# Keys and values with a head pair's two heads on separate halves of the partitions, in a linear-attention plus MoE kernel

## The chip, the cores and the metric

The kernel runs on one core of one Trainium2 chip. The metric is the device time of one execution in microseconds (us). Each run also leaves a profile: a trace of one execution, whose span (first to last instruction) is about 2 us shorter than the device time. A core has these engines: PE (TensorE, matmuls), PEld (the weight loads that go with them), DVE (VectorE), ACT (ScalarE), POOL (GpSimd) and SP, which only issues DMA transfers.

## The reference, cut to what matters

```python
# q, k, v: [8 batches, 8 heads, 576 tokens, 64]   w_in: [512, 2048]   w_out: [2048, 512]   float32
q_s = softmax(q, axis=-1)                    # over the 64 channels of a token
k_s = softmax(k, axis=2)                     # over the 576 tokens, for each channel
kv  = einsum('bhsd,bhse->bhde', k_s, v)      # 64 x 64 per head
x   = einsum('bhsd,bhde->bhse', q_s, kv)     # then heads side by side: 4608 tokens x 512
h   = x @ w_in
out = (h * sigmoid(beta * h)) @ w_out     # 4608 x 512
```

The two products with `w_in` and `w_out` are almost all of the arithmetic. The attention is small, but its results `x` are what the products start from.

## The kernel before

The tokens are worked through in nine slabs of 512: slab t is the first 512 tokens of batch t, and slab 8 holds the 64 remaining tokens of all eight batches. A slab has two passes. Pass 1 makes `GT = silu(beta * (x @ w_in))`, 16 tiles of four matmuls (128x512 each); pass 2 makes `GT @ w_out` (with `w_out` divided by `beta` beforehand), 64 matmuls of the same size. The attention of batches 2 to 7 is slipped in between these matmuls. The attention of batch 0 (the "head" of the kernel, before slab 0) and of batch 1 (between slab 0 and slab 1) can't be hidden, because nothing else is ready for PE.

Heads are worked on in four pairs (`hp`). Before the change both heads of a pair lie on the same 128 partitions, four tokens on each, and the 64 tokens that do not fit (576 - 512) are a remainder of their own, loaded with a separate transfer of 256-byte runs:

```python
def load_main(name, th, bufs, b, split=1): ...     # 512 tokens, runs of 4*64 floats = 1024 bytes
def load_rem(name, th, bufs, b): ...               # 64 tokens, runs of 64 floats = 256 bytes

def exp_main(name, srcb, dstb, b, hp0, n):         # one ACT operation per pair, 128x512
    ...
def kv_rows(b, hp, j):                             # j = 0..3 the main rows, j = 4 the remainder
    ...
    # one matmul: 128 key columns (two heads) times 128 value columns (two heads) plus a column of ones
mm(PS[bk][:, 256 * n:256 * n + 129], l, r_[:, 0:129], j == 0, j == 4, ...)
```

The 128x128 product holds the two heads' 64x64 blocks on its diagonal and useless cross products off it. A mask removes those while the result leaves PSUM, and `RC` (one over the sum of the key exponentials) normalises it:

```python
def kvd(b, hp, bk, c):
    add(DVE, lambda e: e.scalar_tensor_tensor(
        KVD[i][:, hp, :], PS[bk][:, c:c + 128], RC[i][:, hp:hp + 1], MASK[:, :],
        ALU.mult, ALU.mult), ...)
```

For batches 0 and 1, which PE waits for, the order is this. `ksum` forms the key sums ahead of the values, with one-column matmuls; then, pair by pair, the values, `KVD`, the product with the transposed q (`QT`), and the copy to `XT`, which is what `w_in` is multiplied with:

```python
def values_now(b, pool, acts):
    for hp in range(NHP + 1):
        if hp < NHP:
            for j in range(5):  mm(PS[bk][:, 0:128], l, r_[:, 0:128], ...)   # values of pair hp
            kvd(b, hp, bk, 0)                                                # DVE
        if hp:
            go(out_step(b, hp - 1, pool, ACTE if hp - 1 in acts else DVE))   # PE, then ACT or DVE
```

`warm(n, bank)` issues n filler matmuls whose result nobody reads; they are meant to keep PE's granted clock up. The program gives each engine one list of instructions, in the order of the code.

The softmax here doesn't subtract the row's maximum and nothing guards it: scores larger than these inputs give would overflow.

Of the kernel before, what the change touches and what calls it, by code (L numbers as in the profile page):

```python
# [12 lines left out]
H = 8  # L13
S = 576
# [10 lines left out]
VW = 2 * D + 2  # L25
# [128 lines left out]
def bass_efficient_attn_shen__then__act_swish_beta_kernel(  # L154
# [12 lines left out]
    with ExitStack() as es:  # L167
# [7 lines left out]
        KF = [sb(f"KF{i}", [128, H, 4, D], F32) for i in range(2)]  # L175
        VF = [sb(f"VF{i}", [128, H, 4, D], F32) for i in range(2)]
        QRF = sb("QRF", [128, H, D], F32)
        KRF = [sb(f"KRF{i}", [128, H, D], F32) for i in range(2)]
        VRF = [sb(f"VRF{i}", [128, H, D], F32) for i in range(2)]
        EQ = [sb(f"EQ{i}", [128, NHP, 4, 2, D], BF16) for i in range(2)]  # L180
        EK = [sb(f"EK{i}", [128, NHP, 4, 2, D], BF16) for i in range(2)]
        EQR = sb("EQR", [128, H, D], BF16)
        EKR = [sb(f"EKR{i}", [128, H, D], BF16) for i in range(2)]
# [4 lines left out]
        VB = [sb(f"VB{i}", [128, 4, NHP, VW], BF16) for i in range(2)]  # L188
        VR = [sb(f"VR{i}", [128, NHP, VW], BF16) for i in range(2)]
# [18 lines left out]
        MASK = sb("MASK", [128, 128], F32)  # L208
# [21 lines left out]
        add(DVE, lambda e: e.memset(MASK[:, :], 0.0), w=["mask0"])  # L230
        add(DVE, lambda e: e.memset(MASK[0:64, 0:64], 1.0), r=["mask0"], w=["mask1"])
        add(DVE, lambda e: e.memset(MASK[64:128, 64:128], 1.0), r=["mask0"], w=["mask2"])

        def homes(i):
            add(POOL, lambda e: e.memset(VB[i][:, :, :, 2 * D:VW], 1.0), w=[("vone", i)])
            for p in (0, 32, 64, 96):
                add(POOL, lambda e, p=p: e.memset(
                    VR[i][p:p + 32, :, 2 * D:VW], 1.0 if 32 <= p < 96 else 0.0),
                    w=[("vrone", i, p)])
            for p in (0, 96):  # L240
                add(POOL, lambda e, p=p: e.memset(KRF[i][p:p + 32, :, :], 0.0), w=[("krf0", i, p)])
                add(POOL, lambda e, p=p: e.memset(VRF[i][p:p + 32, :, :], 0.0), w=[("vrf0", i, p)])

# [17 lines left out]
        def load_rem(name, th, bufs, b):  # L261
            i = b % 2
            a = bass.AP(th, b * H * S * D + SM * D, [[D, SR], [S * D, H], [1, D]])
            add(SP, lambda e: e.dma_start(bufs[i][32:96, :, :], a), w=[(name, i)],
                slot=f"{name}{i}")
# [7 lines left out]
        def load_k(b, split=1):  # L273
            load_rem("krf", kt_h, KRF, b)
            load_main("kf", kt_h, KF, b, split)

        def load_v(b, split=1):
            load_rem("vrf", vt_h, VRF, b)
            load_main("vf", vt_h, VF, b, split)

# [8 lines left out]
        def exp_main(name, srcb, dstb, b, hp0, n):  # L289
            i = b % 2  # L290
            for hp in range(hp0, hp0 + n):
                o = bass.AP(dstb[i], hp * 512, [[2048, 128], [64, 2], [128, 4], [1, 64]])
                a = bass.AP(srcb[i], hp * 512, [[2048, 128], [256, 2], [64, 4], [1, 64]])
                add(ACTE, lambda e, o=o, a=a: e.activation(o, a, ACT.Exp),  # L294
                    r=[(name + "f", i, hp)], w=[("e" + name, i, hp)])

        def exp_q(b, hp0=0, n=4):
            exp_main("q", QF, EQ, b, hp0, n)

        def exp_k(b, hp0=0, n=4):  # L300
            exp_main("k", KF, EK, b, hp0, n)

        def exp_kr(b):
            i = b % 2
            add(ACTE, lambda e: e.activation(EKR[i][:, :, :], KRF[i][:, :, :], ACT.Exp),
                r=[("krf", i), ("krf0", i, 0), ("krf0", i, 96)], w=[("ekr", i)])
# [25 lines left out]
        def cast_v(b, hp, eng=POOL):  # L332
            i = b % 2
            o = bass.AP(VB[i], hp * VW, [[4 * NHP * VW, 128], [NHP * VW, 4], [64, 2], [1, 64]])
            a = bass.AP(VF[i], hp * 512, [[2048, 128], [64, 4], [256, 2], [1, 64]])
            add(eng, lambda e: (e.copy if eng == ACTE else e.tensor_copy)(o, a),  # L336
                r=[("vf", i, hp), ("vone", i)], w=[("vb", i, hp)])

        def cast_vr(b, eng=POOL):
            i = b % 2  # L340
            o = bass.AP(VR[i], 0, [[NHP * VW, 128], [VW, NHP], [1, 2 * D]])
            a = bass.AP(VRF[i], 0, [[H * D, 128], [2 * D, NHP], [1, 2 * D]])
            add(eng, lambda e: e.tensor_copy(o, a),  # L343
                r=[("vrf", i), ("vrf0", i, 0), ("vrf0", i, 96)], w=[("vr", i)])
# [35 lines left out]
        def kv_rows(b, hp, j):  # L380
            i = b % 2
            if j < 4:
                return (bass.AP(EK[i], hp * 512 + j * 128, [[2048, 128], [1, 128]]),
                        VB[i][:, j, hp, :], [("ek", i, hp)], [("vb", i, hp)], [("vone", i)])
            return (bass.AP(EKR[i], hp * 128, [[512, 128], [1, 128]]), VR[i][:, hp, :],
                    [("ekr", i)], [("vr", i)], [("vrone", i, p) for p in (0, 32, 64, 96)])

        def kvd(b, hp, bk, c):
            i = b % 2
            add(DVE, lambda e: e.scalar_tensor_tensor(  # L390
                KVD[i][:, hp, :], PS[bk][:, c:c + 128], RC[i][:, hp:hp + 1], MASK[:, :],
                ALU.mult, ALU.mult),
                r=[("ps", bk), ("rc", i, hp), "mask0", "mask1", "mask2"], w=[("kvd", i, hp)],
                bank=[bk])

        def kv_steps(b, hps, pool=MB):
# [3 lines left out]
            def one(n, hp, j):  # L400
                if n == 0 and j == 0:
                    st["b"] = bank(pool)
                bk = st["b"]
                l, r_, ke, kv, ko = kv_rows(b, hp, j)
                mm(PS[bk][:, 256 * n:256 * n + 129], l, r_[:, 0:129], j == 0, j == 4,
                   r=ke + kv, w=[("ps", bk)], bk=bk)
                if n == len(hps) - 1 and j == 4:
                    for m, h2 in enumerate(hps):
                        s_ = PS[bk][:, 256 * m + 128:256 * m + 129]
                        add(DVE, lambda e, s_=s_, h2=h2: e.reciprocal(RC[i][:, h2:h2 + 1], s_),  # L410
                            r=[("ps", bk)], w=[("rc", i, h2)], bank=[bk])
                        kvd(b, h2, bk, 256 * m)
            return [lambda n=n, hp=hp, j=j: one(n, hp, j) for n, hp in enumerate(hps)
                    for j in range(5)]

        def out_mm(b, hp, bk):
            i = b % 2
            mm(PS[bk][:, :], KVD[i][:, hp, :], QT[i][:, hp, :], True, True,
               r=[("kvd", i, hp), ("qt", i, hp)], w=[("ps", bk)], bk=bk)
# [41 lines left out]
        def outr_steps(b):  # L461
# [3 lines left out]
            def one(hp, e_):  # L465
                if hp == 0 and e_ == 0:
# [4 lines left out]
                   True, True, r=[("kvd", e_, hp), "qtr"], w=[("ps", bk)], bk=bk)  # L471
# [6 lines left out]
        def attn(b):  # L478
            s = spread(kv_steps(b, (0, 1)) + kv_steps(b, (2, 3)), 8, 36)
# [26 lines left out]
        def ksum(b, hp, kb):  # L506
            for j in range(5):
                l, r_, ke, kv, ko = kv_rows(b, hp, j)
                mm(PS[kb][:, hp:hp + 1], l, r_[:, 128:129], j == 0, j == 4, r=ke + ko,
# [7 lines left out]
        def values_now(b, pool, acts):  # L517
            i = b % 2
            for hp in range(NHP + 1):
                if hp < NHP:  # L520
                    bk = bank(pool)
                    for j in range(5):
                        l, r_, ke, kv, ko = kv_rows(b, hp, j)
                        mm(PS[bk][:, 0:128], l, r_[:, 0:128], j == 0, j == 4, r=ke + kv,
# [32 lines left out]
        wgate = []  # L557
        warm(8, 0)
        exp_q(0)
        for hp in range(NHP):  # L560
            norm_main(0, hp, 1, POOL if hp % 2 else DVE)
        for c in range(8):
            a = bass.AP(win_h, 256 * c, [[DFF, 128], [128 * DFF, NM], [1, 256]])
            add(POOL, lambda e, c=c, a=a: e.dma_start(WIN[:, :, 256 * c:256 * c + 256], a),
                w=[("win", c)], slot=f"win{c}", after=P.writer[("kf", 0, 3)] if c == 0 else ())
            if c == 1:
                cast_vr(0)
            if c == 4:
                wgate.append(P.ops[-1])
        homes(1)  # L570
        kb = bank(HEAD)
        go(t_steps(0, (0,), HEAD, ACTE))
        warm(3, 0)
        go(t_steps(0, (1,), HEAD, ACTE))
        warm(2, 0)
        exp_kr(0)
        exp_k(0, 0, 1)
        go(t_steps(0, (2,), HEAD, ACTE))
        warm(3, 0)
        exp_k(0, 1, 2)  # L580
        ksum(0, 0, kb)
        warm(3, 0)
        ksum(0, 1, kb)
        warm(1, 0)
        go(t_steps(0, (3,), HEAD, ACTE))
        warm(2, 0)
        bb = bank(HEAD)
        mm(PS[bb][:, 0:NF], BT[:, :], IDF[:, :], True, True, r=["bt", "idf"], w=[("ps", bb)],
           bk=bb, tr=True)
        add(DVE, lambda e: e.tensor_scalar(BC[:, :], PS[bb][:, 0:NF], -1e-20, None, ALU.is_gt),  # L590
            r=[("ps", bb)], w=["bc0"], bank=[bb])
        add(DVE, lambda e: e.scalar_tensor_tensor(BC[:, :], PS[bb][:, 0:NF], 1e-20, BC[:, :],
                                                  ALU.is_lt, ALU.mult),
            r=[("ps", bb), "bc0"], w=["bc"], bank=[bb])
        add(DVE, lambda e: e.scalar_tensor_tensor(BETA[:, :], BC[:, :], 4e-20, PS[bb][:, 0:NF],
# [183 lines left out]
```

## Time and profile before

Median 292.86 us (292.64 to 292.89). The profiled execution has a span of 290.5 us.

| | before |
|---|---|
| start of the values of batch 0 | 14.29 us |
| first matmul of slab 0's pass 1 / pass 2 | 17.11 / 31.27 us |
| key sums of batch 1, start | 45.98 us |
| values of batch 1, start | 47.56 us |
| first matmul of slab 1 | 51.21 us |
| last matmul | 286.24 us |
| landing of the last chunk of Q, K, V of batch 0 | 6.56, 10.70, 14.09 us |

All times are from the start of the span. (The 6.75 us that the prediction below gives for Q is the landing of the small `beta` load just behind it.) First the page of the profile: busy time, share of the span and number of instructions of each engine; the DMA packets by size; and the chain of work that ended last, by engine.

```profile
PE 281.4 (97%) x1499; PEld 133.1 (46%) x1499; DVE 114.0 (39%) x225; ACT 165.9 (57%) x251; POOL 44.1 (15%) x77
...
DMA packets 58291, 47.32 MB, mean 163 GB/s; under 512 B 26001, under 2 KB 54689, under 8 KB 57249
...
PE 94%; DVE 2%; DMA 1%; ACT 0%; POOL 0%; issue 0%; POOLq 0%
```

The kernel is bound by PE: the chain is PE for 94%. A change can then win only by giving PE less to do, or by making PE wait less where it does wait, and these places are the head and batch 1's attention.

Next, some groups of instructions by their shapes: line, engine, operation, output<-input, shapes and count, then the busy time in us and the mean duration in ns, then the idle time before them.

```profile
L357 PE MATMUL PS<-WOUT,GT 128*128 128x512 bf16 x576 | 133.2, 379 | 0.0
L357 PE MATMUL PS<-XT,WIN 128*128 128x512 bf16 x576 | 132.3, 379 | 0.8 <-ACT XT L427 0.7
...
L357 PE MATMUL PS<-VB,EK 128*128 128x129 bf16 x96 | 20.3, 220 | 0.0
...
L294 ACT ACTIVATE EK<-KF 128x512 bf16<-128x512 f32 x32 | 18.0, 617 | 0.6 <-DMA KF<-in_k_dram 0.2
...
L390 DVE SCALAR_TENSOR_TENSOR KVD<-PS,RC,MASK 128x128 bf16<-128x128 f32 x32 | 10.9, 349 | 2.1 <-PE PS L357 1.0
```

A mean duration is not the cost of one more instruction where instructions overlap. The large matmuls last 379 ns each but start every 216 ns; a 129-column matmul lasts 220 ns and adds 57 ns. For that reason costs below are differences of start times, and PE's busy time, a sum of overlapping stretches, is not used.

The key exponentials of batch 0 on ACT and the two ends of slab 0's pass 1 on PE, from the timeline (start, length of the merged stretch, engine, line, what, count):

```profile
9.75 0.62 ACT L294 ACTIVATE EK<-KF 128x512 bf16<-128x512 f32 x1
...
10.73 1.16 ACT L294 ACTIVATE EK<-KF 128x512 bf16<-128x512 f32 x2
...
13.10 0.63 ACT L294 ACTIVATE EK<-KF 128x512 bf16<-128x512 f32 x1
...
17.11 14.33 PE L357 MATMUL PS<-XT,WIN 128*128 128x512 bf16 x64
...
31.27 4.91 PE L357 MATMUL PS<-WOUT,GT 128*128 128x512 bf16 x22
```

And batch 1's attention: the end of the key sums, the fillers, the start of the values, slab 1.

```profile
46.46 0.16 PE L357 MATMUL PS<-VR,EKR 128*128 128x1 bf16 x1
46.49 1.24 PE L357 MATMUL PS<-WARM 128*128 128x512 bf16 x5
47.56 0.39 PE L357 MATMUL PS<-VB,EK 128*128 128x128 bf16 x4
...
51.21 3.01 PE L357 MATMUL PS<-XT,WIN 128*128 128x512 bf16 x13 [0.68 <-ACT XT L427]
```

### The profile page before, as it was taken

The page shows a single profiled execution, that of the slowest core. Times are in us where ns is not written, and L with a number is a line of the kernel's source. Part 1 is how long each engine was busy: PE and PEld are TensorE (multiplying, and loading weights), DVE is VectorE, ACT ScalarE, POOL GpSimd, SP SyncE. Part 2 cuts the span into 40 slices and gives each one's busy share as a digit, 9 for nine tenths or more (in the row PEclk, how much of TensorE's full clock was granted, in tenths as well). Part 3 has the DMA queues.
Part 4 walks back from the last instruction along what each step waited for, and adds up shares of the span by engine and source line. Part 5 has one row for each costly group of instructions (what it writes and reads, how often), then busy time and mean ns, then how long its engine had stood idle before and what let it go on. Part 6 is the DMA issues. An engine that isn't in the chain of part 4 may idle for free.

```text
span 290.5 us, 3750 instructions
## 1 busy us (share of the span) xinstructions
PE 281.4 (97%) x1499; PEld 133.1 (46%) x1499; DVE 114.0 (39%) x225; ACT 165.9 (57%) x251; POOL 44.1 (15%) x77
## 2 busy tenths in 40 slices
PE   6899998999999999999999999999999999999994
PEld 2444445444545444544454445444544444444441
DVE  4430596215686046505580557044904400110011
ACT  5777572979767852787268716891670086017500
POOL 5780015034541300210012000000000000000000
PEclk9799999999999999999999999999999999999999
DMA  6999999999999989506980016000900030012022
GB/s 200 306 179 318 383 327 292 343 363 286 323 337 322 204 246 347 96 2 186 331 225 2 1 54 165 0 1 18 206 13 0 2 144 0 2 54 90 0 74 72
DMA packets 58291, 47.32 MB, mean 163 GB/s; under 512 B 26001, under 2 KB 54689, under 8 KB 57249
## 3 DMA queue, kind: packets, MB, share of 16 engines
q1 hardware_dynamic: 53728, 44.45, 52.1%
q0 software_dynamic: 4224, 2.10, 5.6%
q10 hardware_dynamic: 320, 0.52, 0.6%
q8 instruction: 12, 0.20, 0.3%
q14 instruction: 7, 0.05, 0.1%
HBM read 36.71 MB, written 9.44 MB: 159 GB/s over the span
## 4 chain that ended last, share of the span: by engine, by line
PE 94%; DVE 2%; DMA 1%; ACT 0%; POOL 0%; issue 0%; POOLq 0%
PE PS L357 93%; PE PS L355 1%; DMA QF<-in_q_dram 1%; DVE XT L427 1%; DVE QS L319 0%; DVE KVD L390 0%; POOL EQ L321 0%; DVE O2S L633 0%; DVE EQ L321 0%; ACT EQ L294 0%; ACT XT L427 0%; DVE QI L320 0%; POOLq L137 0%
## 5 line engine op out<-in xcount | busy, mean ns | idle before, releaser
L628 ACT ACTIVATE GT<-PS,BETA 128x512 bf16<-128x512 f32 x144 | 98.5, 687 | 87.6 <-PE PS L357 87.6
L357 PE MATMUL PS<-WOUT,GT 128*128 128x512 bf16 x576 | 133.2, 379 | 0.0
L357 PE MATMUL PS<-XT,WIN 128*128 128x512 bf16 x576 | 132.3, 379 | 0.8 <-ACT XT L427 0.7
L357 PEld LDWEIGHTS PS<-WOUT,GT 128*128 128x128 bf16 x576 | 54.5, 98 | 62.3
L357 PEld LDWEIGHTS PS<-XT,WIN 128*128 128x128 bf16 x576 | 53.5, 98 | 62.3 <-ACT XT L427 1.0
L633 DVE COPY O2S<-PS 128x512 f32<-128x512 f32 x34 | 23.3, 688 | 112.9 <-PE PS L357 112.8
L357 PE MATMUL PS<-VB,EK 128*128 128x129 bf16 (+2 forms) x160 | 24.9, 209 | 0.0
L319 DVE TENSOR_REDUCE QS<-EQ 128x8 f32<-128x512 bf16 (+1 forms) x22 | 20.0, 909 | 7.7 <-ACT EQ L294 7.7
L427 DVE CAST XT<-PS 128x512 bf16<-128x512 f32 x27 | 18.6, 690 | 11.3 <-PE PS L357 11.2
L294 ACT ACTIVATE EQ<-QF 128x512 bf16<-128x512 f32 x32 | 18.1, 620 | 6.7 <-DMA QF<-in_q_dram 6.3
L336 POOL CAST VB<-VF 128x512 bf16<-128x512 f32 x28 | 18.1, 648 | 9.5 <-DMA VF<-in_v_dram 7.4
L294 ACT ACTIVATE EK<-KF 128x512 bf16<-128x512 f32 x32 | 18.0, 617 | 0.6 <-DMA KF<-in_k_dram 0.2
L357 PEld LDWEIGHTS PS<-VB,EK 128*128 128x128 bf16 x160 | 13.2, 98 | 8.7 <-ACT EK L294 0.7
L321 DVE TENSOR_TENSOR EQ<-EQ,QI 128x1024 bf16<-128x1024 bf16 (+1 forms) x14 | 15.8, 1129 | 0.5
L343 POOL CAST VR<-VRF 128x512 bf16<-128x512 f32 x8 | 4.9, 616 | 66.4 <-PE PS L357 53.4
L321 POOL TENSOR_TENSOR EQ<-EQ,QI 128x512 bf16<-128x512 bf16 x8 | 8.3, 1043 | 32.1 <-DVE QI L320 31.9
L357 PE MATMUL PS<-QT,KVD 128*128 128x512 bf16 x32 | 11.9, 381 | 0.7 <-DVE KVD L390 0.7
L357 PE MATMUL PS<-WARM 128*128 128x512 bf16 x30 | 10.7, 481 | 1.2 <-DVE WARM L221 1.2
L390 DVE SCALAR_TENSOR_TENSOR KVD<-PS,RC,MASK 128x128 bf16<-128x128 f32 x32 | 10.9, 349 | 2.1 <-PE PS L357 1.0
L355 PE MATMUL PS<-IDB,EQ 128*128 128x128 bf16 x48 | 6.3, 234 | 2.5 <-DVE EQ L321 1.6
L357 PE MATMUL PS<-VR,EKR 128*128 128x129 bf16 (+2 forms) x40 | 8.2, 208 | 0.0
L551 DVE TENSOR_SCALAR WOUT<-WST,RB 128x512 bf16<-128x512 f32 x8 | 3.3, 482 | 11.6 <-DMA WST<-in_moe_w_out_dram 11.6
(55 smaller groups left out, 98.9 us busy)
## 6 DMA issues: line engine op xcount, KB each, us to landing
out_dram<-O2S SPq DMA_DIRECT2D x8, 1024.0 KB, 5.1
QF<-in_q_dram SPq DMA_DIRECT2D x6, 1024.0 KB, 8.5
KF<-in_k_dram SPq DMA_DIRECT2D x6, 1024.0 KB, 8.8
VF<-in_v_dram SPq DMA_DIRECT2D x6, 1024.0 KB, 8.8
QF<-in_q_dram SPq DMA_DIRECT2D x8, 256.0 KB, 6.9
KF<-in_k_dram SPq DMA_DIRECT2D x8, 256.0 KB, 5.6
VF<-in_v_dram SPq DMA_DIRECT2D x8, 256.0 KB, 5.7
WIN<-in_moe_w_in_dram POOLq DMA_DIRECT2D x8, 256.0 KB, 6.3
```

Of the source, the lines that this page charges most:

```text
L294: add(ACTE, lambda e, o=o, a=a: e.activation(o, a, ACT.Exp), r=[(name + "f", i, hp)], w=[("e" + name, i, hp)])
L319: add(DVE, lambda e: e.tensor_reduce(s_, a, AX.X, ALU.add), r=ks, w=[("qs", i, hp0)])
L321: add(eng, lambda e: e.tensor_tensor(a, a, vb, ALU.mult), r=ks + [("qi", i, hp0)], w=ks)
L336: add(eng, lambda e: (e.copy if eng == ACTE else e.tensor_copy)(o, a), r=[("vf", i, hp), ("vone", i)], w=[("vb", i, hp)])
L343: add(eng, lambda e: e.tensor_copy(o, a), r=[("vrf", i), ("vrf0", i, 0), ("vrf0", i, 96)], w=[("vr", i)])
L355: add(PE, lambda e: e.transpose(o, l, r_), r=r, w=w, bank=[bk])
L357: add(PE, lambda e: e.matmul(o, l, r_, start=start, stop=stop), r=r, w=w, bank=[bk])
L390: add(DVE, lambda e: e.scalar_tensor_tensor(KVD[i][:, hp, :], PS[bk][:, c:c + 128], RC[i][:, hp:hp + 1], MASK[:, :], ALU.mult, ALU.mult), ...
L427: add(eng, lambda e: (e.copy if eng == ACTE else e.tensor_copy)(XT[i][:, hp, :], PS[bk][:, :]), r=[("ps", bk)], w=[("xt", i, hp)], bank=[bk])
L551: add(DVE, lambda e, f=f: e.tensor_scalar(WOUT[:, f, :], STAGE[c][:, f % 4, :], RB[:, f:f + 1], None, ALU.mult), r=SKEY[c] + ["rb"], w=[(" ...
L628: add(ACTE, lambda e: e.activation(GT[:, f, :], PS[bk][:, :], ACT.Silu, scale=BETA[:, f:f + 1]), r=[("ps", bk), "beta"], w=[("gt", f)], ba ...
L633: add(eng, lambda e: (e.copy if eng == ACTE else e.tensor_copy)(O2S[t % 2][:, u, :], PS[bk][:, :]), r=[("ps", bk)], w=[("o2", t % 2, u)], ...
```

## The change

The two heads of a pair go to 64 partitions each, nine tokens on every partition (64 x 9 = 576). There is no remainder of keys or values any more, and the runs in memory are 2304 bytes long. To keep the heads apart in one matmul, the key exponentials are written block-diagonally into a tile that is zero elsewhere: the upper head into columns 0 to 63, the lower into 64 to 127. The product then has only 64 value columns, and no mask is needed. Cut to its core:

```diff
-VW = 2 * D + 2
+NG = S // 64
+VW = D + 2
+KW = NG * D
@@
-        EK = [sb(f"EK{i}", [128, NHP, 4, 2, D], BF16) for i in range(2)]
+        EK = [sb(f"EK{i}", [128, NHP, NG, 2 * D], BF16) for i in range(2)]
@@ (homes) zeros off the diagonal, once, on POOL
+                z = EK[i][64 * e_:64 * e_ + 64, :, :, 64 * (1 - e_):64 * (2 - e_)]
+                add(POOL, lambda e, z=z: e.memset(z.bitcast(F32), 0.0), w=[("ekz", i, e_)])
@@ (exp_k) two operations of 64 partitions per pair; step=2 (two pairs at once) from batch 2 on
+            for hp in range(hp0, hp0 + n, step):
+                hps = range(hp, hp + step)
+                for e_ in range(2):
+                    o = bass.AP(EK[i], 64 * e_ * NHP * NG * 128 + hp * NG * 128 + 64 * e_,
+                                [[NHP * NG * 128, 64], [128, NG * step], [1, 64]])
+                    a = bass.AP(KF[i], 64 * e_ * NHP * KW + hp * KW,
+                                [[NHP * KW, 64], [64, NG * step], [1, 64]])
+                    add(ACTE, lambda e, o=o, a=a: e.activation(o, a, ACT.Exp), ...)
@@ (kvd) two operations of 64 partitions in place of one masked one per pair; from batch 2 on
@@       one such operation covers two or four pairs
+            for e_ in range(2):
+                o = bass.AP(KVD[i], 64 * e_ * NHP * 128 + hp * 128 + 64 * e_, ...)
+                add(DVE, lambda e, o=o, a=a, s_=s_: e.tensor_tensor(o, a, s_, ALU.mult), ...)
@@ (kv_steps, ksum, values_now) nine matmuls per pair in place of five, of half the width
-                mm(PS[bk][:, 256 * n:256 * n + 129], l, r_[:, 0:129], j == 0, j == 4, ...)
+                mm(PS[bk][:, VW * n:VW * n + D + 1], l, r_[:, 0:D + 1], j == 0, j == NG - 1, ...)
@@ (head) two w_in loads issued one key chunk earlier, ahead of Q's last pair on POOL;
@@        q transposes copied by DVE, one V cast more on DVE, all XT copies on ACT, four fillers fewer
+        load_win(0)
+        load_win(1)
...
-        values_now(0, HEAD, (1, 3))
+        values_now(0, HEAD, (0, 1, 2, 3))
```

## The prediction

It was written before anything of the change was built or run.

> **What bounds the kernel.** The chain of waits is PE for 94% of a 290.5 us span. In the two large products a 128x512 matmul starts every 216 ns (matmul starts in the trace); 1152 of them, 249 us, are untouched. From 17.8 to 286.6 us PE is fed without a gap except around batch 1's attention (45.8 to 51.2 us, 4.3 us busy). Only the head (0 to 17.8 us) and the attention matmuls between the large ones can give.
>
> **Matmuls.** Per batch 20 matmuls of 129 columns become 36 of 65. In the trace a 129-column one adds 57 ns between large ones; a 64-column one (QTR,KVD) 28 ns; the weight load stays hidden in both. So 20 x 57 = 1.14 us becomes 36 x 29 = 1.04 us: about 0.6 us over six batches. The key sums of batches 0 and 1 are one-column matmuls at 25 ns; 36 instead of 20 cost 0.4 us more each. The Trainium skill (page "TensorE: Matmul & The Clock Gate", section "Back-to-back issue gap") gives a floor of about 25 ns; the trace agrees. On PE alone: nearly nothing.
>
> **ScalarE.** Back to back, a 512-element exponential takes 0.52 us, a 1-element one 0.20 us: about 0.1 us plus 0.83 ns per element. Half-filled partitions double the elements: keys cost 8 x 0.58 = 4.6 us in batches 0 and 1 and 4 x 1.06 = 4.2 us later, against 2.6 us with the remainder. ScalarE is 57% busy; only slab 1's second pass is tight (two batches' exponentials, 66.5 to 77.8 us before; to about 81.4 after on the old clock, just when the last XT copy is wanted). At most 0.3 us lost there.
>
> **DMA and head.** The head is a stream of loads: Q has landed at 6.75, K at 10.70, V at 14.09 us; the first full product starts at about 17.8 us. Runs of 1024 B move 256 KB in 0.75 us (350 GB/s), the 256 B remainders 128 KB in 0.50 us (262 GB/s), the w_out loads with 2048 B runs 1 MB in 2.7 us (387 GB/s). With 2304 B runs and no remainders K and V should take about 3.0 us each: V lands at 12.8 to 13.3 us. ScalarE loses four QT copies to DVE but gains 2 us of exponentials, which end near 12.3 us (13.7 before). Mask memsets, remainder casts and four filler matmuls leave; all XT copies go to ScalarE, so DVE no longer holds up KVD. I estimate the first full product near 16.2 us: 1.6 us saved.
>
> **Batch 1.** Its loads land about 2 us earlier, so they keep up with the earlier PE; its key exponentials end just when slab 0's second pass does. Key sums +0.4 us, perhaps 0.1 us for the last pair's EQ.
>
> **Sum.** -1.6 (head) +0.5 (batch 1) -0.6 (interleaved) +0.1 (slab 1) = -1.6 us: 291.2 us, range 289.8 to 292.6. Chances: faster by over 2% 0.02, within 2% 0.96, slower 0.02.
>
> **What would show it.** Start to first full product shorter by 1 to 2 us; V landing before 13.5 us; starts after a 65-column matmul spaced near 29 ns; ScalarE busy time up by about 13 us without PE waiting for it; DMA packets from 58,000 to about 42,000; the rest within 0.5 us of before.
>
> **What would make it wrong.** The granted clock is 0.5 from 7.6 to 11.0 us after a thin stretch; fewer fillers could move or add such a stretch (up to +1.7 us). PE waiting for key exponentials in batches 0 or 1, or slab 2's first activations delayed. The w_in loads, issued one key chunk earlier, could slow V. Half-partition operations could cost more than the same columns on 128.

## More of the kernel before

```profile
48.04 0.63 DVE L390 SCALAR_TENSOR_TENSOR KVD<-PS,RC,MASK 128x128 bf16<-128x128 f32 x2 [1.00 <-PE PS L357]
...
49.49 0.60 DVE L390 SCALAR_TENSOR_TENSOR KVD<-PS,RC,MASK 128x128 bf16<-128x128 f32 x2
```

Two masked KVD operations take 0.60 us together although one lasts 0.35: the second starts before the first has ended.

## The result, and the profile after

The changed kernel took 293.83 us (293.14 to 294.42, four runs) against 292.86 us (four runs with the one of that round). Ratios here are the mean time of one kernel's fast runs over that of the other's in the same rounds, so not quite the ratio of the medians quoted: 1.0029, 95% interval 1.0011 to 1.0047. It is within 2%, as forecast, but slower and not faster, and outside the predicted range of 289.8 to 292.6 us. A second set of six runs on another chip (e6 below) gave 1.0013 (0.9991 to 1.0034). The honest result is "nothing gained, perhaps 0.1 to 0.3% lost".

The same lines of the page for the changed kernel, whose profiled span is 292.0 us:

```profile
PE 279.4 (96%) x1623; PEld 133.5 (46%) x1655; DVE 112.1 (38%) x206; ACT 181.5 (62%) x248; POOL 42.3 (14%) x61
...
DMA packets 41652, 47.33 MB, mean 162 GB/s; under 512 B 17553, under 2 KB 29857, under 8 KB 40609
...
PE 81%; DMA 8%; SPq 4%; ACT 2%; POOL 1%; issue 1%; DVE 1%
```

The packets fell as forecast. ACT became 15.6 us busier. The chain is no longer 94% PE: loads, and ACT's exponentials, now stand in it. The groups:

```profile
L346 PE MATMUL PS<-VB,EK 128*128 128x65 bf16 x216 | 32.2, 193 | 0.4
L301 ACT ACTIVATE EK<-KF 64x1152 bf16<-64x1152 f32 x24 | 27.8, 1158 | 0.4
...
L301 ACT ACTIVATE EK<-KF 64x576 bf16<-64x576 f32 x16 | 10.9, 681 | 2.3 <-DMA KF<-in_k_dram 2.0
...
L383 DVE TENSOR_TENSOR KVD<-PS,RC 64x64 bf16<-64x64 f32 x16 | 3.6, 222 | 2.1 <-PE PS L346 1.7
```

The head:

```profile
8.20 5.62 ACT L301 ACTIVATE EK<-KF 64x576 bf16<-64x576 f32 x8 [0.39 <-DMA KF<-in_k_dram]
...
17.36 14.33 PE L346 MATMUL PS<-XT,WIN 128*128 128x512 bf16 x63
...
31.53 4.70 PE L346 MATMUL PS<-WOUT,GT 128*128 128x512 bf16 x21
```

The eight exponentials follow each other without a pause for 5.62 us, 0.70 to 0.71 us from start to start, and end at 13.82 us. In the kernel before they ended at 13.73 us although they began 1.5 us later. Batch 1's attention, PE and then DVE:

```profile
46.23 1.25 PE L346 MATMUL PS<-VB,EK 128*128 128x1 bf16 x36
47.35 1.24 PE L346 MATMUL PS<-WARM 128*128 128x512 bf16 x5
48.43 0.71 PE L346 MATMUL PS<-VB,EK 128*128 128x64 bf16 x18
...
52.77 1.47 PE L346 MATMUL PS<-XT,WIN 128*128 128x512 bf16 x6 [0.68 <-ACT XT L421]
```

```profile
48.93 0.98 DVE L383 TENSOR_TENSOR KVD<-PS,RC 64x64 bf16<-64x64 f32 x4 [1.08 <-PE PS L346]
...
50.67 0.98 DVE L383 TENSOR_TENSOR KVD<-PS,RC 64x64 bf16<-64x64 f32 x4
```

The four half KVD operations of two pairs take 0.98 us, where two masked ones took 0.60 to 0.63: one lasts 0.22 us, and they start 0.25 us apart. They do not overlap at all.

So the two profiled executions differ, stage by stage (starts of matmuls in the traces):

| stage | before, us | after, us | difference |
|---|---|---|---|
| to slab 0's pass 2 (the head, and pass 1 of slab 0) | 31.27 | 31.53 | +0.26 |
| pass 2 of slab 0, to batch 1's key sums | 14.71 | 14.70 | -0.01 |
| key sums of batch 1 (start to the first filler) | 0.51 | 1.12 | +0.61 |
| fillers | 1.07 | 1.08 | +0.01 |
| values of batch 1 to the first matmul of slab 1 | 3.65 | 4.34 | +0.69 |
| slab 1, pass 1 | 14.36 | 14.48 | +0.12 |
| slab 1, pass 2, to the last matmul | 220.67 | 220.49 | -0.18 |
| sum (last matmul) | 286.24 | 287.74 | +1.50 |

In these two traces the loss is made up of the attention of batches 0 and 1; the whole rest gains 0.06 us. One trace is one execution: in a second trace of the changed kernel (e6 below) slab 0's pass 2 starts at 31.03 us, 0.24 us before the kernel before, so the sign of the head's term is not shown. That the forecast 1.6 us were not gained is.

### The profile page after: what moved, and what is told of

It reads as the page before. It is cut to its first block, busy times and chain, and to the rows that moved or that the text cites. A ratio compares the mean times of both kernels' runs of the same rounds, so it can differ in the third digit from the quotient of the medians.

```text
span 292.0 us, 3977 instructions
## 1 busy us (share of the span) xinstructions
PE 279.4 (96%) x1623; PEld 133.5 (46%) x1655; DVE 112.1 (38%) x206; ACT 181.5 (62%) x248; POOL 42.3 (14%) x61
## 2 busy tenths in 40 slices
DMA packets 41652, 47.33 MB, mean 162 GB/s; under 512 B 17553, under 2 KB 29857, under 8 KB 40609
## 4 chain that ended last, share of the span: by engine, by line
PE 81%; DMA 8%; SPq 4%; ACT 2%; POOL 1%; issue 1%; DVE 1%
PE PS L346 81%; DMA KF<-in_k_dram 5%; SPq L251 3%; DMA WIN<-in_moe_w_in_dram 2%; ACT EK L301 2%; SPq L540 1%; POOL WIN L555 1%; DVE KVD L383 1%; PE PS L344 0%; POOL EQ L317 0%; SPq L261 0%; DVE O2S L633 0%; ACT XT L421 0%; SPq L530 0%
## 5 line engine op out<-in xcount | busy, mean ns | idle before, releaser
L346 PE MATMUL PS<-WOUT,GT 128*128 128x512 bf16 x562 | 131.8, 379 | 0.6
L346 PEld LDWEIGHTS PS<-XT,WIN 128*128 128x128 bf16 x576 | 54.9, 98 | 63.1 <-ACT XT L421 1.6
L301 ACT ACTIVATE EK<-KF 64x1152 bf16<-64x1152 f32 (+1 forms) x40 | 38.7, 967 | 2.7 <-DMA KF<-in_k_dram 2.0
L346 PE MATMUL PS<-VB,EK 128*128 128x65 bf16 (+2 forms) x360 | 38.1, 187 | 1.9 <-ACT EK L301 0.8
L332 POOL CAST VB<-VF 128x576 bf16<-128x576 f32 x28 | 21.2, 757 | 74.4 <-DMA VF<-in_v_dram 42.4
L346 PEld LDWEIGHTS PS<-VB,EK 128*128 128x128 bf16 x360 | 24.2, 97 | 9.6 <-ACT EK L301 1.4
L421 DVE CAST XT<-PS 128x512 bf16<-128x512 f32 x25 | 17.2, 691 | 11.0 <-PE PS L346 10.9
L346 PE MATMUL PS<-QT,KVD 128*128 128x512 bf16 x29 | 11.1, 381 | 1.3 <-DVE KVD L383 0.9
L346 PE MATMUL PS<-WARM 128*128 128x512 bf16 x25 | 9.1, 483 | 1.2 <-DVE WARM L219 1.2
L383 DVE TENSOR_TENSOR KVD<-PS,RC 64x64 bf16<-64x64 f32 (+2 forms) x30 | 8.9, 298 | 2.5 <-PE PS L346 1.7
L344 PEld LDWEIGHTS PS<-IDB,EQ 128*128 128x128 bf16 x48 | 4.1, 105 | 6.2 <-issue 2.4
```

Source lines behind the costliest of these rows:

```text
L301: add(ACTE, lambda e, o=o, a=a: e.activation(o, a, ACT.Exp), r=[("kf", i, h) for h in hps], w=[("ek", i, h, e_) for h in hps])
L332: add(eng, lambda e: (e.copy if eng == ACTE else e.tensor_copy)(o, a), r=[("vf", i, hp), ("vone", i)], w=[("vb", i, hp)])
L344: add(PE, lambda e: e.transpose(o, l, r_), r=r, w=w, bank=[bk])
L346: add(PE, lambda e: e.matmul(o, l, r_, start=start, stop=stop), r=r, w=w, bank=[bk])
L383: add(DVE, lambda e, o=o, a=a, s_=s_: e.tensor_tensor(o, a, s_, ALU.mult), r=[("ps", bk)] + [("rc", i, h) for h in hps], w=[("kvd", i, h, ...
L421: add(eng, lambda e: (e.copy if eng == ACTE else e.tensor_copy)(XT[i][:, hp, :], PS[bk][:, :]), r=[("ps", bk)], w=[("xt", i, hp)], bank=[bk])
```

## The experiments

Theories at the start. S: the half-filled exponentials on ScalarE hold up the key sums. K: the halved KVD operations on VectorE lengthen the chain from values to XT. D: batch 1's first key chunk lands late (in the changed kernel at 41.41 us, where 15 of its 16 parts had landed by 39.93) and holds up everything behind it.

The table holds the stages of the traces that the argument uses, in us from the start of the span. One trace is one execution; the same changed kernel (after, e6) differs by 0.5 us between its two. The runs e1 to e4 had one chip, e6 to e9 another, the f and g runs a third. Two columns hardly move between traces of one kernel and carry most of the argument: "values 1 to slab 1" (V1) and "values 0 to the head's end" (V0; the head's end is the start of slab 0's pass 2 less the 13.82 us that 64 matmuls of 216 ns take, so it is right only where pass 1 does not stall). V0 also takes in waits for other things than KVD: for `w_in` and RC in f1 (0.19 and 0.39 us), for `w_in` in e1 (0.41 us), for RC in f3 (0.71 us).

| run | values 0 | pass 2 of slab 0 | key sums 1 | values 1 | slab 1 | last matmul | V0 | V1 |
|---|---|---|---|---|---|---|---|---|
| before | 14.29 | 31.27 | 45.98 | 47.56 | 51.21 | 286.24 | 3.16 | 3.65 |
| after | 14.33 | 31.53 | 46.23 | 48.43 | 52.77 | 287.74 | 3.38 | 4.34 |
| e6, after again | 13.83 | 31.03 | 45.93 | 48.05 | 52.40 | 287.36 | 3.38 | 4.35 |
| e1, one exponential per pair | 13.64 | 31.07 | 47.16 | 49.14 | 53.49 | 288.34 | 3.61 | 4.35 |
| e2, masked KVD | 14.20 | 31.13 | 45.84 | 47.96 | 51.63 | 286.60 | 3.11 | 3.67 |
| e3, before with halved exponentials | 16.59 | 33.58 | 48.29 | 49.87 | 53.52 | 288.67 | 3.17 | 3.65 |
| f1, masked KVD, zigzag | 13.91 | 31.24 | 47.59 | 50.05 | 53.73 | 288.57 | 3.51 | 3.68 |
| f2, f1 without fillers | 13.57 | 30.51 | 45.29 | 47.22 | 50.90 | 285.74 | 3.12 | 3.68 |
| f3, e1 with Q's last pair first | 12.71 | 30.62 | 45.79 | 47.77 | 52.12 | 286.97 | 4.09 | 4.35 |
| f4, f3 with half of w_out | 12.14 | 30.32 | 45.02 | 47.01 | 51.35 | 286.20 | 4.36 | 4.34 |
| g1, before without fillers | 14.11 | 31.15 | 46.12 | 47.11 | 50.87 | 285.89 | 3.22 | 3.76 |
| g2, f2 again | 14.05 | 30.98 | 46.49 | 47.51 | 51.40 | 286.24 | 3.11 | 3.89 |

### e1: one exponential per key pair

```diff
-                for e_ in range(2):      # batches 0 and 1: two operations on 64 partitions
+                o = bass.AP(EK[i], hp * NG * 128, [[NHP * NG * 128, 128], [128, NG], [1, 64]])
+                a = bass.AP(KF[i], hp * KW, [[NHP * KW, 128], [64, NG], [1, 64]])   # 128 partitions
```

The lower head's exponentials land in the wrong columns, so the result is wrong (the tile's other columns are set to ones to keep sums finite).

> The changed kernel with the key exponentials of batches 0 and 1 as four operations on 128 partitions (576 elements each) in place of eight on 64; the result is wrong on purpose, every later operation stays. Theory S (ScalarE: half-filled exponentials hold up the key sums): exponentials of batch 0 end near 11.2 us instead of 13.8, those of batch 1 near 44.5 instead of 47.1; the first full product starts about 1.0 us earlier than in the changed kernel (18.2 us), the first product of slab 1 about 1.8 us earlier (52.8 us), in all near 292.0 us. Rival K (only the doubled KVD operations on VectorE cost): less than 0.3 us gained, near 293.6 us. Rival D (a late first key chunk of batch 1 from DMA, last of 16 engines at 41.4 us): no gain in batch 1 beyond what the head gives.

Measured: 293.90 us, ratio 1.0013 (0.9979 to 1.0046). Batch 0's exponentials ended at 11.00 us instead of 13.82, and batch 1's at 45.03 instead of 47.05. So the part of S about ScalarE is right, and yet hardly anything was gained. In the head the values started only 0.69 us earlier (0.19 us earlier than in e6): the transposes of Q's last pair, whose normalisation POOL does after issuing two `w_in` loads, were ready at 12.69 us only, and behind the values PE waited for the first `w_in` chunk, which in this run landed at 17.20 us. In batch 1 a wait appeared that the changed kernel did not have, as the timeline of PE shows:

```profile
43.50 0.40 PE L353 MATMUL PS<-IDB,EQ 128*128 128x128 bf16 x4 [0.76 <-POOL EQ L326]
...
46.06 0.40 PE L353 MATMUL PS<-IDB,EQ 128*128 128x128 bf16 x4 [0.22 <-POOL EQ L326]
```

PE waits for the normalised Q of batch 1 (EQ), which came late because the loads were late. Theory S alone falls: the exponentials are one of several paths of nearly equal length.

### e2: KVD of a pair in one masked operation

```diff
+            if n == 1:                                   # batches 0 and 1
+                a = bass.AP(PS[bk], c, [[512, 128], [0, 2], [1, 64]])   # the 64 columns, read twice
+                m = bass.AP(MASK, 0, [[128, 128], [64, 2], [1, 64]])
+                add(DVE, lambda e: e.scalar_tensor_tensor(
+                    o, a, RC[i][:, hp:hp + 1], m, ALU.mult, ALU.mult), ...)
```

> The changed kernel with KVD of one pair made by one masked operation on 128 partitions, reading the 64 PSUM columns twice, as the kernel before does with 128 columns; only in the attention of batches 0 and 1; the result is right. Rival K (KVD in two halves, 0.25 us each, not overlapped, in the chain values-KVD-output-XT): each of the two stages shorter by 0.3 to 0.5 us, total near 293.0 us. If KVD is not on the chain: same as the changed kernel, 293.8 us. Theory S alone (ScalarE) expects at most 0.2 us.

Measured: 293.14 us, ratio 0.9992 (0.9956 to 1.0029), result right. From the DVE timeline and the PE timeline of batch 1:

```profile
48.47 0.66 DVE L387 SCALAR_TENSOR_TENSOR KVD<-PS,RC,MASK 128x128 bf16<-128x128 f32 x2 [1.01 <-PE PS L351]
```

```profile
51.64 2.55 PE L351 MATMUL PS<-XT,WIN 128*128 128x512 bf16 x11 [0.68 <-ACT XT L436]
```

V1 is 3.67 us, that of the kernel before, against 4.34 or 4.35 in every trace that has the halves; V0 is 3.11 against 3.38. f2 and g2 below, with the masked KVD too, have V0 of 3.12 and 3.11. Theory K holds: halving KVD costs 0.68 us in batch 1 and 0.27 us in the head, 0.95 us in all. The sign of the total agrees, but the interval of the time is wider than the effect; the stages show it, not the totals.

### e3: the kernel before with its key exponentials halved

```diff
-                o = bass.AP(dstb[i], hp * 512, [[2048, 128], [64, 2], [128, 4], [1, 64]])
+            for e_ in range(2):                          # batches 0 and 1
+                p = 64 * e_ * 2048
+                o = bass.AP(EK[i], p + hp * 512, [[2048, 64], [64, 2], [128, 4], [1, 64]])
```

> The kernel before with one part of the change alone: the key exponentials of batches 0 and 1 each split into two operations on 64 partitions (512 elements, dense layout, right result). Theory S: 8 x 0.65 us or so in place of 4 x 0.52 to 0.62; head longer by 1.5 to 2.3 us (first full product 19.3 to 20 us instead of 17.8), batch 1 hardly longer since its keys land 0.6 us earlier there (0 to 0.4 us); total near 294.6 us (+0.6%). If half-filled exponentials are harmless: 292.9 us.

Measured: 294.78 us, ratio 1.0049 (1.0019 to 1.0079). The values of batch 0 started at 16.59 us instead of 14.29, and from there on each stage was as before, but for 0.12 us in slab 1's first pass. In the ACT timeline two of these exponentials merge into 1.27 us:

```profile
9.50 1.27 ACT L311 ACTIVATE EK<-KF 64x512 bf16<-64x512 f32 x2
```

One of them lasts 627 ns, so they did not overlap. In the head of the kernel before, halving costs 2.3 us. The changed kernel offsets most of this by starting the exponentials 1.5 us earlier (no key remainder, and no QT copies on ACT).

### e4: the exponentials ordered by half

```diff
-            for hp in range(hp0, hp0 + n, step):
-                hps = range(hp, hp + step)
-                for e_ in range(2):
+            for e_ in range(2):
+                for hp in range(hp0, hp0 + n, step):
```

> The changed kernel with the key exponentials of a batch ordered by half: all of partitions 0 to 63, then all of 64 to 127, right result. If it is the change of the partition half from one operation to the next that stops two operations from overlapping: starts within one half are spaced 0.58 us (576 elements) and 1.07 us (1152) in place of 0.706 and 1.18. If half-filled operations never overlap: 0.70 and 1.18 stay. Time within 0.5 us of the changed kernel either way.

The four exponentials of a later batch, in the changed kernel and then in e4:

```profile
103.26 4.70 ACT L301 ACTIVATE EK<-KF 64x1152 bf16<-64x1152 f32 x4
```

```profile
105.27 4.44 ACT L301 ACTIVATE EK<-KF 64x1152 bf16<-64x1152 f32 x4
```

Start to start, e4's are 1.06 us apart within a half and 1.17 us where the half changes; the changed kernel's are always 1.18 us apart. In batch 0 the second half's follow each other at 0.57 to 0.59 us, and the changed kernel's at 0.70. So it is the change of the start partition from one operation to the next that costs 0.11 to 0.13 us, not the half-filled operation as such. The time was 295.83 us in its single run, about 2 us more than the changed kernel, against the expectation: batch 0's first key sums now wait for the second half, and the records of the granted clock show 0.5 from 14.0 to 17.4 us, in the middle of the values.

### e6: the changed kernel again; e7, e8, e9: three versions with an edit too many

e6 is the changed kernel itself, run as a control on the chip of e7 to e9.

> The changed kernel as it is, run again as a control beside the next three on their chip. Expected 293.9 us (ratio to before near 1.003), with the values of batch 0 starting near 14.3 us and the first product of slab 1 at 52.8 us, as in its first trace; how far these move tells how much one trace is worth.

Measured: 293.56 us, ratio 1.0013 (0.9991 to 1.0034); slab 1 started at 52.40 us. V0 and V1 repeat to 0.01 us; the rest moved by 0.3 to 0.5 us. The exponentials of batch 0 took 5.62 us again, and began and ended 0.50 us earlier (7.70 and 13.32 us), because the first key chunk landed at 7.67 us instead of 8.18; the values followed, at 13.83 instead of 14.33.

The three others shared an edit that was meant to bring batch 1's loads forward: the first `w_out` load waits for the third `w_in` chunk instead of the fifth (`if c == 2` in place of `if c == 4` where the gate is set). e7 is e1 with it and with Q's last pair normalised ahead of the `w_in` loads, e8 has the masked KVD and the zigzag order of f1 below, and e9 is e8 without the five fillers.

> The run with one exponential per key pair (wrong on purpose), and two more waits taken away: GpSimd normalises Q's last pair ahead of the first w_in loads, and the w_out loads follow the third w_in load, not the fifth. Theory P (three paths of nearly equal length end in the head's values: key exponentials, Q's last pair on GpSimd, V's last chunk; and two in batch 1: key exponentials, and the load stream w_in, w_out, Q): values of batch 0 start near 12.5 to 13.0 us (14.3 changed kernel, 13.6 with the one exponential alone); first product of slab 1 near 51.7 us (53.5 with the one exponential alone); total near 292.3 us. If the exponentials were the only cause, the two extra edits do nothing: values at 13.6, slab 1 at 53.5, 293.9 us.

> The changed kernel, right result, with the causes mended that earlier runs showed: KVD of one pair in one masked operation, key exponentials in an order that changes the partition half four times per batch instead of seven, w_out loads behind the third w_in load. Expected: exponentials of batch 0 end near 13.4 us (13.8), values start near 13.9 us, values to first product of slab 1 3.67 us (4.35), that product near 51.2 us (before 51.2, changed 52.8); total 0.2 to 0.9 us under the changed kernel, about equal to before (ratio 0.998 to 1.001).

> The last one without the five filler matmuls between batch 1's key sums and values. If the fillers, not the V casts, hold the values there: 1.0 us more saved, the first product of slab 1 near 50.2 us, total near 292.1 us, ratio to before near 0.997. If V's last chunk or the clock holds them: nothing, or a stretch at half clock shows.

Measured: 295.86, 294.66 and 294.32 us, ratios 1.0079, 1.0053 and 1.0036. All three missed for one reason, which e8's list of PE's waits shows (us in total, times, longest):

```profile
PE PS L351 <- DMA WIN<-in_moe_w_in_dram: 2.8, 2, 2.4
```

The `w_out` loads took bandwidth from the `w_in` loads, and slab 0's pass 1 starved. I had thought that the `w_in` stage left bandwidth free. It does not: the profile's DMA queue counts 2.1 MB for it, which is what it writes as bf16, but it reads 4.2 MB of fp32 (36.7 MB read from HBM in all are Q, K and V with 28.3, and the two weights with 4.2 each). In e8 its last chunk landed at 32.19 us, instead of 25.30. The early part of e7 is still of use: with the exponentials and Q's last pair both out of the way, the values started at 12.57 us (predicted there: 12.5 to 13.0).

### f1 and f2: the two mends without that edit

f1 is the changed kernel with e2's KVD and with

```diff
-                for e_ in range(2):
+                for e_ in ((0, 1), (1, 0))[hp // step % 2]:      # "zigzag"
```

and f2 leaves out `warm(5, 3)` ahead of batch 1's values as well.

> The changed kernel, right result, with two mends and the w_out loads where they were (moving them up starved the w_in loads: PE stalled over 3 us in slab 0): KVD of one pair in one masked operation, and key exponentials in the order that changes the partition half four times. Theory (KVD halves and exponentials that do not overlap are most of the loss): values to first product of slab 1 3.67 us, that product at 51.2 to 51.6 us, total 0.7 to 1.1 us under the changed kernel, ratio to before 0.997 to 1.000. If the control's closeness to before (1.0013) means that there is nothing to mend: ratio 1.001.

> The last one without the five filler matmuls between batch 1's key sums and values (1.08 us of PE). If the fillers hold the values: 0.9 to 1.1 us less, first product of slab 1 near 50.4 us, ratio near 0.995. If V's last chunk (48 us) and its cast hold them: 0.3 to 0.5 us less.

f1: 293.60 us, ratio 0.9996 (0.9967 to 1.0025). f2: 292.29 us, ratio 0.9962 (0.9931 to 0.9993), the first version whose interval lies below 1 (its repeat, g2 below, does not confirm that). In f1's trace the third chunk of batch 1's Q landed 2.3 us after the second (0.75 us is usual), and PE stood idle 0.72 and 0.58 us for EQ because of it; the trace shows the same V1 of 3.68 us as e2. In f2 the eight exponentials of the head took 5.22 us instead of 5.62, 0.13 us for each of the three changes of half (seven before, four now) that are gone. Without the fillers PE did not start the values at once; it waited 0.66 us for ACT's copies of the output from PSUM, which stand behind the exponentials in ACT's order:

```profile
47.23 0.70 PE L351 MATMUL PS<-VB,EK 128*128 128x64 bf16 x18 [0.66 <-ACT O2S L648]
```

### f3 and f4: is the stream of loads a second limit?

f3 is e1 with POOL's order changed, and f4 is f3 with two of the four `w_out` loads left out (both wrong):

```diff
-        load_win(0)
-        load_win(1)
@@  after norm_main(0, 3, 1, POOL)
-        for c in range(2, 8):
+        for c in range(8):
@@  f4 only
-        for c in range(4):
+        for c in range(2):
             load_wout(c)
```

> One exponential per key pair in batches 0 and 1 (wrong on purpose) and Q's last pair normalised ahead of the first w_in loads; the w_out loads stay where they were. Head: values start near 12.6 us, first product of slab 0 at 16.2 to 16.8 us. Theory L (the load stream Q,K,V, w_in, w_out, Q,K,V runs without a gap, so the last pairs of batch 1's Q are ready no sooner, whatever the head gains): PE waits for EQ in slab 0's second pass, first product of slab 1 no earlier than 52.0 us, total 292.8 us or more. If the stream is not a limit: 34.9 us after the head's end, 51.3 us, total near 291.9 us.

> The last one with two of the four w_out loads left out (2.1 MB of the stream, 5.4 us; wrong on purpose, the scaling reads the first two again). Theory L: batch 1's Q, K and V land about 5 us earlier, PE no longer waits for EQ, first product of slab 1 near 51.3 us, 0.7 us or more below the last one. If the stream is not a limit: the same as the last one.

f3: 293.45 us, ratio 0.9993 (0.9966 to 1.0020). f4: 292.83 us, ratio 0.9972 (0.9944 to 1.0001). In f3 values began 1.1 to 1.6 us earlier than in the changed kernel's two traces, but the head's end came only 0.4 to 0.9 us earlier (DVE, still casting V, gave the reciprocals late: PE waited 0.7 us for RC). Pass 2 of slab 0 then took 15.17 us to the key sums instead of 14.71, with PE waiting for EQ, and slab 1 started at 52.12 us, as theory L had it. With the lighter stream the same stage took 14.70 us and slab 1 started at 51.35. Theory L holds: with a faster head, batch 1's loads take back 0.46 us. In the changed kernel's own two traces L costs little: pass 2 took 14.70 us in the first, with no such wait, and 14.90 us in e6, whose head ended 0.5 us earlier. It is what a better head runs into.

### g1, g2, g3, g4: what was still open

g1 is the kernel before without `warm(5, 3)`, and g2 is f2 again.

> The kernel before without the five filler matmuls between batch 1's key sums and values; right result. If the fillers hold the values there, as in the mended version: values start 0.5 to 1.1 us sooner, ratio near 0.997, and the mended version's gain is the fillers', not the change's. If V's casts hold them there (V's last chunk lands at 47.4 us, its cast ends at 48.1): ratio 0.999 to 1.000, and the gain is the change's.

> The mended version (masked KVD, key exponentials in the order with fewer changes of half, no fillers) again, on the chip of the kernel before without fillers. Expected ratio 0.996, as measured.

g1: 292.51 us, ratio 0.9985 (0.9955 to 1.0014). g2: 292.04 us, ratio 0.9970 (0.9938 to 1.0002). Both stand within each other's interval. The mended version may be 0.1 to 0.2% better than the kernel before with the same edit, but these runs do not show it. How much of f2's gain is the fillers' stays open too: g1's interval takes in both nothing and f2's 0.9962.

g3 makes the exponentials dense on 128 partitions (four operations) and lets DVE copy the halves into the block-diagonal tile; it also has the masked KVD, POOL's order of f3, and no fillers.

```diff
+                add(ACTE, lambda e, hp=hp, a=a: e.activation(EKD[:, hp, :], a, ACT.Exp), ...)
+            for e_ in range(2):                                    # spread_k
+                add(DVE, lambda e, o=o, a=a: e.tensor_copy(o, a), r=[("ekd", hp)], ...)
```

> The mended version with the key exponentials of batches 0 and 1 dense on 128 partitions (four operations) and spread to the block diagonal by VectorE copies, Q's last pair normalised ahead of the first w_in loads, one V cast moved to ScalarE; right result. Expected: values of batch 0 start near 12.6 us (13.6), first product of slab 0 near 15.7 us (16.3), slab 1 0.2 to 0.6 us sooner than the mended version since the load stream takes back part; ratio near 0.994. If VectorE's copies hold up its other work: no better than the mended version.

Measured: 296.76 us, ratio 1.0142 (1.0106 to 1.0178). ACT was done early, but the sixteen copies of 64x576 elements last 0.44 us each on DVE, which also has the normalisation, the V cast and KVD to do:

```profile
PE PS L369 <- DVE EK L312: 3.2, 5, 1.4
```

The wait moved from ACT to DVE and grew.

g4 tests where the late key chunk comes from. In the changed kernel the DMA records hold a 16 KB packet of the instruction queue at 39.0 us, which took 1.1 us; in the kernel before the packet of that place comes at 47.1 us. g4 makes one matmul per pair in place of nine in batch 0's key sums (wrong), 64 PE instructions fewer, to move it.

```diff
-            for j in range(NG):
+            nj = NG if b else 1
+            for j in range(nj):
```

> The changed kernel with one matmul per pair in place of nine in batch 0's key sums (wrong on purpose): 64 fewer PE instructions. If the last-engine lag of batch 1's first key chunk (1.2 to 2.3 us behind the middle one) comes from the 16 KB instruction fetch at 38.8 to 39.0 us: the fetch moves to 43 to 45 us, and the chunk's last part lands within 0.9 us of its middle one, near 40.4 us. If not: fetch moved, lag unchanged.

The packet moved, but to 28.5 us and not to 43 to 45. The landing records (of the 16 parts of a transfer: the 15th and the 16th to land, us) show what followed:

```
                                     after (packet at 39.0)   g4 (packet at 28.5)
w_out, second load                        30.70   30.77            30.12   31.77
w_out, last load                          36.14   36.22            35.53   37.20
Q of batch 1, last chunk                  39.13   39.20            38.54   40.21
K of batch 1, first chunk                 39.93   41.41            39.30   40.96
V of batch 1, first chunk                 42.96   44.81            42.81   43.98
```

In both, right after the packet one part of sixteen falls 1.5 to 1.7 us behind the others, and it is still 1.2 to 1.9 us behind at the first V chunk; in g4 that is 15 us later. The records do not name the engine of a part, but the lag moved with the packet, which speaks for D's cause: one of the parallel DMA engines is behind from the instruction fetch on. It adds to differences that are there anyway: in e6, with the packet at 38.8 us, the first key chunk's last part came 0.4 us behind the 15th and 1.2 us behind the 8th. f1 fits too: its packet came at 39.85 us, and a part that had been 1.1 us behind the 15th was 2.7 us behind it at the next chunk to land, the late third chunk of Q. That the packet holds up this part is inferred from the times. And it is not worth much in the changed kernel: g4's exponentials of batch 1 began at 40.99 us instead of 41.43, and slab 1 started at 52.52 us against 52.40 and 52.77.

## Why the prediction was wrong

The prediction put -1.6 us in the head, +0.5 us in batch 1, -0.6 us in the interleaved matmuls and +0.1 us in slab 1. Measured, on the two profiled executions: +0.26, +1.30, -0.18 and +0.12 us. The second trace of the changed kernel (e6) has -0.24 us in the head.

**The head (-1.6, measured +0.26, in e6 -0.24; the step that failed).** Three of its claims were right or nearly so. V's last chunk landed at 13.37 us (12.8 to 13.3 predicted, 14.09 before). ACT lost the QT copies and could start sooner. The packets fell to 41,652 (42,000). What failed is "8 x 0.58 = 4.6 us ... which end near 12.3 us": they took 5.62 us and ended at 13.82 us. The 0.58 came from exponentials on 128 partitions that overlap their neighbours by 0.09 us; those of the changed kernel alternate between partition 0 and partition 64 and don't overlap (e4). That is 1.0 us of error, and in e6, where they began at 7.70 us as the forecast implies, it is all of it: they ended at 13.32 us. In the first trace another 0.5 us is their start, at 8.20 us: the first key chunk landed at 8.18 us, no sooner than before (8.17), and Q's last chunk later (7.16, before 6.56). Thus the values started at 14.33 us (13.83 in e6) where about 13 was needed. And even with the exponentials shortened (e1), two further paths end close to where they ended: Q's last pair on POOL at 12.7 us, and V's casts (f3). I had treated the head as one chain with one limit; it is three chains within about 1 us of each other.

**KVD (not in the sum at all).** The prediction removed the mask, and left the two halved operations out of the sum, as if they cost no more than the one they replace: "Half-partition operations could cost more than the same columns on 128" stands only among the risks. They cost about 0.25 us more per pair, in a chain that PE waits for: 0.27 us in the head, 0.68 us in batch 1 (e2). This could have been read beforehand. The Trainium skill, page "VectorE: DVE Perf Modes", section "Two Vector instructions with no wait between them", gives a model by which an instruction whose input or output starts in another quadrant (a group of 32 partitions) than the last one "starts only when every earlier Vector instruction has finished". The trace agrees: halves 0.22 us long start 0.25 us apart, while masked operations 0.35 us long, all from partition 0, start 0.26 to 0.28 us apart (batch 1, before).

**Batch 1 (+0.5, measured +1.30).** The key sums cost 0.40 us more by their number, as predicted (36 x 25 ns, no wait in f4: 0.91 us against 0.51), and another 0.2 us (0.13 us in e6) because PE waited for the last exponentials, which ended at 47.05 us. That they would "end just when slab 0's second pass does" needed both the 0.58 us and loads 2 us earlier. The loads in front were hardly earlier: the last `w_out` load landed at 36.22 us against 36.48, batch 1's last Q chunk at 39.20 against 39.56. Half of the first key chunk was earlier (8 of its 16 parts at 39.09 us against 40.33), but the last part, which counts, came at 41.41 against 40.83 (g4 tests why). The Trainium skill, page "DMA: Bandwidth & Descriptors", section "Why a DMA increments its semaphore by 16 and not by 1", says that a transfer runs on up to 16 engines that finish independently, and that only the full count means landed; this trace shows by how much the last can differ. The largest term is KVD's 0.68 us.

**The interleaved matmuls (-0.6, measured -0.18).** Mechanism right, size off. A 65-column matmul does add 29 to 30 ns, with its weight load hidden. But a pass with nine matmuls per pair fell from 14.95 to 14.91 us only: it has 64 x 0.216 = 13.82 us of large matmuls, so the attention's share went from 1.13 to 1.09 us, and 0.10 us had been predicted. The reason is only rounding of 56.5 and 30 ns into 57 and 29, times 20 and 36.

**Slab 1 (+0.1, measured +0.12).** The size agrees by luck; the mechanism does not. The forecast loss was in slab 1's second pass, which took 16.82 us before and 16.80 after. The measured loss is in pass 1 (14.36 to 14.48 us), at one place: 2.38 us into it PE waits for ACT's first `GT`, which is 0.12 us later. The traces show where ACT lost it. Before, the exponential of Q's remainder (EQR) begins 0.10 us before the copy ahead of it ends; after, it begins 0.02 us behind that end:

```profile
50.57 0.59 ACT L427 CAST XT<-PS 128x512 bf16<-128x512 f32 x1 [0.61 <-PE PS L357]
51.05 0.63 ACT L309 ACTIVATE EQR<-QRF 128x512 bf16<-128x512 f32 x1
```

```profile
52.13 0.59 ACT L421 CAST XT<-PS 128x512 bf16<-128x512 f32 x1 [1.15 <-PE PS L346]
52.74 0.63 ACT L305 ACTIVATE EQR<-QRF 128x512 bf16<-128x512 f32 x1
```

All 18 traces divide the same way. Where the last key exponential of batch 1 starts on partition 64 (after, e2, e3, e4, e6, g4), EQR does not overlap and the pass takes 14.48 us; where it starts on partition 0 (the other twelve), EQR overlaps by 0.10 us and the pass takes 14.36 us. So it looks like e4's lost overlap once more, although four copies that read PSUM lie between the two exponentials. No run was made to test it; e3, which puts only the halves into the kernel before, and the zigzag of f1 are the closest to one. ScalarE's +15.6 us (+13 predicted) are otherwise absorbed, as predicted.

**The clock.** The feared stretch at half clock did not decide this result (granted clock 0.5 from 7.3 to 10.7 us after, 7.7 to 11.1 before; e6 has no such stretch, and the same V0 and V1), but in e4 it fell into the values.

What stays open: the size of the total loss, 0.1 to 0.3%, is near the scatter between runs (291.8 to 295.2 us for the kernel before over all rounds), and so is the worth of the mended version against the kernel before without its fillers.

## What to carry to other kernels

Splitting an operation into two that start on different partitions doubles the elements per lane in all and, when the halves alternate, also takes away the overlap with its neighbours; where the chain is short operations, write one masked operation on all partitions instead, or group the halves. Before crediting a gain to a stage in which PE waits, list every chain that ends there and by how much each is shorter than the last: here shortening the longest one (e1) brought the head's values forward by 0.7 us against one trace of the changed kernel and 0.2 us against the other, where 1.0 us was expected, because two more stood right behind it. And where a stream of loads runs without a gap, a faster start upstream is taken back unless the stream is shortened too.

## What the Trainium skill lacked or had wrong

- "ScalarE: Activation LUTs", section "What ACT_TABLE_LOAD costs", says that back-to-back ACTIVATEs overlap by about 93 ns. These runs agree for operations that start on the same partition (128x512: 612 ns long, 519 ns apart), but the overlap is gone when the start changes between partition 0 and 64 (64x576: 681 ns long, 706 ns apart; 64x1152: 1.18 us apart, against 1.06 within one half). The page does not mention the start partition; the page on VectorE does, for VectorE.
- "TensorE: Matmul & The Clock Gate", section "Back-to-back issue gap", gives about 81 ns (N=128) and 131 ns (N=512) per matmul for streams in which each matmul has its own weight load. Here, with a weight load each, they were 56 ns at 128 columns and 216 ns at 512, which is what the page calls the isolated gap. Its floor of about 25 ns agrees (one-column key sums: 25 ns).
- "Runtime: NRT & Kernel Launch", section "Instruction fetch mechanics", does not say what a fetch does to the data transfers of the kernel. After a 16 KB packet of the instruction queue (1.0 to 1.1 us) one part of sixteen of the next transfers landed 1.2 to 1.9 us behind the 15th in two traces (after, g4) and 0.3 to 0.5 us behind it in e6. That the two share a DMA engine is inferred from these times.
